# Moving the q and k fetches between the two spreads of the score operands in the sync queue of an attention and MoE kernel

## The chip, the cores and the metric

One core of one Trainium2 chip. The metric is device microseconds of one launch, the median of three runs. Engines are named as the profile names them: PE (TensorE matmuls), PEld (its weight loads), DVE (VectorE), ACT (ScalarE), POOL (GpSimd), SP (SyncE, which here only issues DMAs). "SPq" in a row is SP's queue of DMA issues.

## The reference

```python
scores = (1/sqrt(D)) * q @ k.T                     # batch 4, 8 heads, 576 rows, D = 64, fp32
bias   = -(cum[:, :, :, None] - cum[:, :, None, :])   # cum = cumsum(max(s, 0))
scores = where(causal, -1e9, scores + minimum(bias, 0))
attn   = softmax(scores)                           # sum + 1e-9
x      = (attn @ v) as 2304 tokens x 512
e      = argmax(x @ w_gate)                        # one of 8 experts per token
y      = gate * sigmoid(x @ w_output_gate) * (relu(x @ w1[e]) @ w2[e])
out    = relu(y @ w_in)**2 @ w_out                 # 512 -> 2048 -> 512
```

## The kernel before

The launch has two parts. The first (up to about 250 us) is attention with the routing; the second is the experts and the last two layers, in which PE is busy almost without a gap. The change is in the first.

Attention works on 16 pairs of heads, pair `pp` = 0 to 15. For every pair the scores need two operand tiles of 128 partitions, one per head: `sta` (three buffers, `st_a`, L312) and `stb` (two buffers, `st_b`, L313). PE transposes q and k (L404, L408), ACT and DVE write high and low parts into `sta` (L434, L438), and then DMAs within the on-chip memory bring the halves to the partitions where the score matmuls (L490) want them:

- **spread b** (`spread_b`, three moves at L441, 576 + 144 + 144 KB) fills `stb` from `sta`;
- **spread a** (`spread_a`, two moves at L441, 144 KB each) copies within `sta`. It writes rows that spread b reads, so its issue waits until spread b has landed;
- `load_aug` (L393, L394) brings four rows of the cumulated bias for each head, ahead of spread b for `stb`, behind spread a for `sta`.

The first score matmul of a pair, `s<-sta` with 68 partitions and 192 columns, needs the last of these, `sta<-aug_d`. In front of it stand only the older instructions of PE.

`load_qk` (L353, L356) fetches raw q and k of a pair from HBM, four DMAs: q and k of 256 KB, and the tails of q and k of 32 KB. They have two buffers each, so the fetch for pair pp waits until POOL has reordered (L373) those of pair pp-2. `load_v` (L380, L383) fetches v in three DMAs, and `store_x` (L726, L730) writes attention's output of an older pair in two. From pair 8 on the first expert's weights come in between, 256 KB a time (`part_load`, `stg`, L253), and ACT rounds them (L257).

All these DMAs are issued by SP, one after another. The order is fixed by numbers: `at(key, function, ...)` collects every step with a key in units (seven units are the seven score blocks of a pair), and each engine gets its instructions in the order of the keys. With `t0 = 7 * pp - 7`, `early` = 7 from pair 5 on, and the table `K_`:

```python
at(max(t0 + K_["ldqk"] - early(pp), t0 - 2 * NU + K_["scq"] - early(pp - 2) + 0.2), load_qk, pp)
tb = t0 + max(K_["dup"], K_["qk"][2] + K_["qkl"] - early(pp) + 0.4)   # t0 - 2.9 from pair 3 on
at(tb - 0.05, load_aug, pp, 1)
at(tb, spread_b, pp)
at(tb - K_["dup"] + K_["dupa"], spread_a, pp)                         # t0 + 0.6 from pair 3 on
at(tb - K_["dup"] + K_["dupa"], load_aug, pp, 0)
```

Of the kernel before, what the change touches and what calls it, by code (L numbers as in the profile page):

```python
# [48 lines left out]
    LE=1.22,  # L49
    LV=0.63,  # L50
    vact=[[0], [1], [1], [1], [0], [1], [1, 1]],
    ldqk=-13.2,
    ldv=-3.41,
    scq=-4.19,
    sck=-5.35,
# [1551 lines left out]
```

## Time and profile before

| | |
|---|---|
| median of 3 runs | 932.81 us (929.98 to 934.12) |
| the profiled execution | 931.6 us, its span 929.7 us |
| PE busy in the span | 867.6 us (93%), 5397 matmuls |
| DVE, ACT, POOL busy | 528.6, 446.3, 283.8 us |
| granted clock of PE, mean | 0.975 |
| DMA, mean | 133 GB/s, 123.87 MB |

All times below are in microseconds from the start of the span of this one execution. A row of a timeline gives the start, the duration, the engine, the line and what was done (x2: two instructions merged in one row), and in brackets the idle time just before it with what ended that. SP's own durations are the time an issue took, not the transfer.

### The profile page before, as it was taken

Reading aid. Unit: us, or ns where it says so; the run is one execution under the profiler, and the core shown is the slowest. Engines: PE = TensorE matmul, PEld = TensorE weight load, DVE = VectorE, ACT = ScalarE, POOL = GpSimd, SP = SyncE. Lnnn points to the kernel's source line nnn. Section 1 sums busy time; section 2 is a strip of 40 time slices with the busy share of each in tenths; the row PEclk is TensorE's granted clock in tenths of the full one; section 3 lists DMA queues with packets and bytes.
Section 4 is the critical chain, followed back from the end, with each engine's and each line's share of the span. In section 5 each row is a group of like instructions: output and inputs, shape, how many; then the busy total and the mean of one; then the engine's idle time right before and its main releaser. Section 6 shows DMA issues by size and latency. Waiting matters only on the chain.

```text
span 929.7 us, 15091 instructions
## 1 busy us (share of the span) xinstructions
PE 867.6 (93%) x5397; PEld 761.8 (82%) x5397; DVE 528.6 (57%) x1166; ACT 446.3 (48%) x985; POOL 283.8 (31%) x311
## 2 busy tenths in 40 slices
PE   7999998889989999998987899999999999999992
PEld 5777766667589989998987798999999999989991
DVE  8777666667758787887695666332323322322220
ACT  6677677778436556555654444232322323222220
POOL 5333143532236577767540244011001001001001
PEclk9999899999999999999998999999999999999996
DMA  5667677777158888888966642220000100000001
GB/s 151 160 155 177 164 172 193 188 191 187 37 181 277 253 251 282 279 232 271 305 221 195 199 151 71 68 68 15 25 29 35 35 1 35 1 1 35 1 1 37
DMA packets 87572, 123.87 MB, mean 133 GB/s; under 512 B 33601, under 2 KB 58177, under 8 KB 86594
## 3 DMA queue, kind: packets, MB, share of 16 engines
q1 hardware_dynamic: 80978, 103.77, 40.4%
q0 software_dynamic: 6224, 18.01, 5.4%
q10 hardware_dynamic: 288, 1.05, 0.4%
q8 instruction: 45, 0.74, 0.3%
q14 instruction: 37, 0.30, 0.1%
HBM read 83.12 MB, written 23.17 MB: 114 GB/s over the span
## 4 chain that ended last, share of the span: by engine, by line
PE 32%; issue 30%; DMA 16%; ACT 6%; DVE 5%; POOL 4%; SPq 3%; POOLq 0%; DVEq 0%; ACTq 0%
PE z L1196 10%; PE z L1241 6%; DMA stb<-sta 4%; PE z L1234 3%; PE s L490 3%; DMA cv<-in_moe_w_in_dram 3%; PE t L588 3%; PE t L550 2%; DVE w L238 2%; ACT p L534 2%; POOL out_dram L1273 2%; DMA sta<-aug_d 1%; DMA cv<-in_moe_w_out_dram 1%; DMA stg<-in_moe_w_dram 1%; SPq L441 1%
## 5 line engine op out<-in xcount | busy, mean ns | idle before, releaser
L1196 PE MATMUL z<-xt,w 128*128 128x384 f32 (+6 forms) x1920 | 338.5, 325 | 6.3 <-DVE r L1214 3.0
L1196 PEld LDWEIGHTS z<-xt,w 128*128 128x128 f32 x1920 | 316.0, 190 | 16.3 <-DVE h L1208 3.4
L1241 PE MATMUL z<-w,h 128*128 128x512 f32 x864 | 214.9, 393 | 0.0
L1241 PEld LDWEIGHTS z<-w,h 128*128 128x128 f32 x864 | 160.7, 188 | 29.3
L1214 DVE SCALAR_TENSOR_TENSOR r<-z,r 128x384 f32<-128x384 f32 x96 | 53.3, 555 | 168.2 <-ACT r L1213 168.2
L1213 ACT ACTIVATE r<-z 128x384 f32<-128x384 f32 x96 | 47.0, 490 | 168.2 <-PE z L1196 166.4
L1234 PE MATMUL z<-h,w 128*128 128x304 f32 (+5 forms) x768 | 117.6, 302 | 8.2 <-ACT h L1207 5.9
L1234 PEld LDWEIGHTS z<-h,w 128*128 128x128 f32 x768 | 109.6, 191 | 9.4 <-ACT h L1207 6.3
L238 DVE TENSOR_TENSOR w<-stg,w 128x1024 fp32r<-128x1024 f32 x72 | 109.8, 1525 | 8.5 <-ACT w L234 8.2
L1273 POOL DMA_INDIRECT out_dram<-ysb,tok_m x18 | 17.4, 964 | 314.7 <-ACT ysb L1260 312.4
L234 ACT CAST w<-stg 128x1024 fp32r<-128x1024 f32 x72 | 75.5, 1049 | 70.5 <-DMA stg<-in_moe_w_dram 50.0
L1217 DVE TENSOR_TENSOR h<-r,h 128x384 fp32r<-128x384 f32 x96 | 56.7, 590 | 55.6 <-ACT h L1216 55.6
L534 ACT ACTIVATE p<-p,nm 128x128 f32<-128x128 f32 (+3 forms) x144 | 84.3, 590 | 4.2 <-DVE nm L517 4.1
L517 DVE CUSTOM_DVE_ANT_0 p<-s,mask 128x128 f32<-128x128 f32 (+3 forms) x128 | 59.8, 486 | 45.9 <-PE s L490 45.0
L1216 ACT CAST h<-r 128x384 fp32r<-128x384 f32 x96 | 49.3, 513 | 73.4 <-DVE r L1214 73.4
L1178 POOL TENSOR_TENSOR cvm<-cvm,cva 128x512 f32<-128x512 f32 x32 | 44.1, 1377 | 100.3 <-DVE cva L1177 59.1
L550 PE MATMUL t<-ident,p 128*128 128x128 f32 x400 | 69.5, 289 | 2.1 <-ACT pt L569 0.7
L490 PE MATMUL s<-sta 68*128 68x192 f32 (+7 forms) x204 | 51.7, 350 | 14.9 <-DMA sta<-aug_d 13.2
L550 PEld LDWEIGHTS t<-ident,p 128*128 128x128 f32 x400 | 47.1, 145 | 15.3 <-ACT p L534 7.2
L1179 POOL TENSOR_TENSOR cvm<-cvs,cvm 128x512 f32<-128x512 f32 x32 | 58.9, 1841 | 2.5
L588 PE MATMUL t<-pt,v 128*64 128x320 f32 (+4 forms) x448 | 53.1, 368 | 0.0
L569 ACT COPY pt<-t 128x512 f32<-128x512 f32 (+1 forms) x94 | 46.8, 514 | 12.2 <-PE t L550 7.1
(218 smaller groups left out, 957.3 us busy)
## 6 DMA issues: line engine op xcount, KB each, us to landing
stg<-in_moe_w_dram SPq DMA_DIRECT2D x56, 512.0 KB
cv<-in_moe_w_out_dram SPq DMA_DIRECT2D x16, 512.0 KB
stb<-sta SPq DMA_DIRECT2D x14, 576.0 KB
cv<-in_moe_w_in_dram SPq DMA_DIRECT2D x14, 512.0 KB
xr<-yT_d SPq DMA_DIRECT2D x6, 768.0 KB
q<-in_q_dram SPq DMA_DIRECT2D x16, 256.0 KB
k<-in_k_dram SPq DMA_DIRECT2D x16, 256.0 KB
v<-in_v_dram SPq DMA_DIRECT2D x32, 128.0 KB
```

The lines of the kernel that those rows point to most:

```text
L234: nc.scalar.copy(out=w_parts(job)[0], in_=raw[job])
L238: nc.vector.tensor_tensor(out=lo, in0=raw.pop(job), in1=hi.bitcast(F32), op=ALU.subtract)
L490: nc.tensor.matmul(ps[0:mw, d0:d0 + nn], lhsT=ql[r, m0:m0 + mw], rhs=kl[r, c0:c0 + nn], start=(i == 0 and (tail or n == 0)), stop=(done an ...
L517: nc.vector.tensor_tensor_reduce(out=dst, in0=src, in1=msk, scale=-1.0, scalar=3.0e38, op0=ALU.add, op1=ALU.min, accum_out=nm[:, c:c + 1])
L534: nc.scalar.activation(out=pt[:, cs], in_=pt[:, cs], func=AF.Exp, scale=-1.0, bias=nm[:, c:c + 1], accum_out=rs[:, r:r + 1])
L550: nc.tensor.transpose(tp[:, i * P:(i + 1) * P], pt[:, j0:j0 + P], ident)
L588: nc.tensor.matmul(o[64 * hd:64 * hd + 64, c0:n], lhsT=vt[r0:P, jb, hd, :], rhs=pt[r0:P, hd, jb, c0:n], start=(jb == 0), stop=(jb == last))
L1179: nc.gpsimd.tensor_tensor(out=m, in0=sq, in1=m, op=ALU.add)
L1196: nc.tensor.matmul(ps[:, 0:n], lhsT=wa[:, zw, kk, fl * P:(fl + 1) * P], rhs=xt[:, zx, kk, 0:n], start=(i == 0), stop=(i == 3 * KD - 1))
L1217: nc.vector.tensor_tensor(out=ht[:, 1, 0:n], in0=gg, in1=ht[:, 0, 0:n].bitcast(F32), op=ALU.subtract)
L1234: nc.tensor.matmul(y_acc[g][d][:, 0:n], lhsT=wb[:, zw, fl, d * P:(d + 1) * P], rhs=ht[:, zh, 0:n], start=(f == 0 and i == 0), stop=(f == n ...
L1241: nc.tensor.matmul(acc, lhsT=ht[:, zh, c * P:(c + 1) * P], rhs=wb[:, zw, fl, :], start=(f == 0 and i == 0), stop=(f == nf - 1 and i == 2))
```

## The change

One number of the table: the key of the q and k fetch.

```diff
-    ldqk=-13.2,
+    ldqk=-16.83,
```

From pair 5 on the key of the fetch for pair pp goes from t0 - 20.2 towards t0 - 23.83. Counted from the pair three earlier, whose t0 is 21 units less, that is from t0 + 0.8 (behind its spread a at t0 + 0.6) to t0 - 2.83 (behind its spread b at t0 - 2.9). The instructions of PE, DVE, ACT and POOL keep their order; on SP the fetches of pairs 6 to 15, 40 DMAs, change place, ten times the same way. The fetches of the pairs before stay where they are.

SP at pair 6, with the fetch for pair 9 (`stb_136`, `sta_133` are the buffers of pair 6):

```order
 L441 DMA stb_136<-sta_133 64x576 x2
+L353 DMA q<-in_q_dram 128x2x256
+L356 DMA q<-in_q_dram 64x2x64
+L353 DMA k<-in_k_dram 128x2x256
+L356 DMA k<-in_k_dram 64x2x64
 L441 DMA sta_133<-sta_133 64x576 x2
 L393 DMA sta_133<-aug_d 4x576
 L394 DMA sta_133<-aug_d 4x576
-L353 DMA q<-in_q_dram 128x2x256
-L356 DMA q<-in_q_dram 64x2x64
-L353 DMA k<-in_k_dram 128x2x256
-L356 DMA k<-in_k_dram 64x2x64
```

The four fetches went from behind the bias rows of `sta` to the place between the last move of spread b and the first of spread a.

SP at pair 9, where weights (`stg`) are fetched too, behind the last move of spread b:

```order
+L353 DMA q<-in_q_dram 128x2x256
+L356 DMA q<-in_q_dram 64x2x64
+L353 DMA k<-in_k_dram 128x2x256
+L356 DMA k<-in_k_dram 64x2x64
 L253 DMA stg<-in_moe_w_dram 128x512
 L441 DMA sta_133<-sta_133 64x576 x2
 L393 DMA sta_133<-aug_d 4x576
 L394 DMA sta_133<-aug_d 4x576
-L353 DMA q<-in_q_dram 128x2x256
-L356 DMA q<-in_q_dram 64x2x64
-L353 DMA k<-in_k_dram 128x2x256
-L356 DMA k<-in_k_dram 64x2x64
```

Here a weight fetch stood between the spreads already; the fetches of q and k now stand ahead of it too.

SP at pair 2 of the kernel before, which has this order of the fetches already, and keeps it:

```order
L441 DMA stb_136<-sta_135 64x576 x2
L353 DMA q<-in_q_dram 128x2x256
L356 DMA q<-in_q_dram 64x2x64
L353 DMA k<-in_k_dram 128x2x256
L356 DMA k<-in_k_dram 64x2x64
L441 DMA sta_135<-sta_135 64x576 x2
L393 DMA sta_135<-aug_d 4x576
L394 DMA sta_135<-aug_d 4x576
L380 DMA v<-in_v_dram 128x4x64 x2
```

Nothing moved here: it is the one place of the kernel before where q and k are fetched between the spreads.

## Rows read from the trace of the kernel before

**Rows 1.** Waits of PE, 30 to 245 us: total, times, longest.

```profile
PE s L490 <- DMA sta<-aug_d: 13.2, 7, 2.8
```

**Rows 2.** Waits of SP's queue, whole span: total, times, longest.

```profile
SPq L441 <- DMA stb<-sta: 20.9, 14, 2.6
...
SPq L353 <- POOL qr L373: 4.6, 1, 4.6
...
SPq L393 <- PE s L490: 2.5, 7, 0.5
```

**Rows 3.** Timeline of SP, one cycle: the DMAs around pair 6.

```profile
86.70 0.43 SPq L393 DMA_DIRECT2D stb<-aug_d  x1
...
87.58 3.60 SPq L441 DMA_DIRECT2D stb<-sta  x3
93.19 1.10 SPq L441 DMA_DIRECT2D sta<-sta  x2
...
94.92 0.25 SPq L394 DMA_DIRECT2D sta<-aug_d  x1
95.26 0.39 SPq L353 DMA_DIRECT2D q<-in_q_dram  x1
...
97.79 1.09 SPq L380 DMA_DIRECT2D v<-in_v_dram  x2
...
99.63 0.54 SPq L726 DMA_DIRECT2D x_d<-xs  x1
...
100.83 0.43 SPq L393 DMA_DIRECT2D stb<-aug_d  x1
```

**Rows 4.** Timeline of PE: the first score matmul of pairs 3, 6, 8, 11, 12, 13.

```profile
54.95 0.45 PE L490 MATMUL s<-sta 68*128 68x192 f32 x2
...
96.89 0.45 PE L490 MATMUL s<-sta 68*128 68x192 f32 x2 [1.68 <-DMA sta<-aug_d]
...
126.38 0.45 PE L490 MATMUL s<-sta 68*128 68x192 f32 x2 [1.58 <-DMA sta<-aug_d]
...
172.85 0.46 PE L490 MATMUL s<-sta 68*128 68x192 f32 x2 [2.69 <-DMA sta<-aug_d]
...
189.19 0.45 PE L490 MATMUL s<-sta 68*128 68x192 f32 x2 [2.42 <-DMA sta<-aug_d]
...
204.68 0.45 PE L490 MATMUL s<-sta 68*128 68x192 f32 x2
```

**Rows 5.** Stretches: length, busy us (instructions) of PE, PEld, DVE, ACT, POOL; clock, DMA share, GB/s.

```profile
86.70:100.83 14.13, 12.39 (x87) 9.24 (x86) 8.96 (x33) 9.21 (x27) 2.83 (x4) 0.91 0.73 170
...
206.00:217.81 11.81, 11.76 (x91) 8.78 (x89) 8.99 (x37) 10.35 (x31) 2.55 (x2) 1.00 0.84 200
...
98.00:105.20 7.20, 7.20 (x35) 5.54 (x33) 5.07 (x22) 5.12 (x17) 3.85 (x5) 0.53 0.83 198
```

**Rows 6.** Timeline of SP around pair 2, whose fetch stands between the spreads already.

```profile
28.92 0.44 SPq L393 DMA_DIRECT2D stb<-aug_d  x1
...
29.80 3.71 SPq L441 DMA_DIRECT2D stb<-sta  x3
33.60 0.72 SPq L353 DMA_DIRECT2D q<-in_q_dram  x1
...
36.55 1.18 SPq L441 DMA_DIRECT2D sta<-sta  x2
...
38.76 2.17 SPq L380 DMA_DIRECT2D v<-in_v_dram  x2
...
42.94 0.41 SPq L393 DMA_DIRECT2D stb<-aug_d  x1
```

**Rows 7.** Timeline of SP, pair 9: weights between the spreads.

```profile
136.37 0.83 SPq L253 DMA_DIRECT2D stg<-in_moe_w_dram  x1
138.35 1.10 SPq L441 DMA_DIRECT2D sta<-sta  x2
```

**Rows 8.** Timeline of ACT: a rounding of weights that waited for their fetch.

```profile
155.72 0.62 ACT L257 CAST w<-stg 128x512 fp32r<-128x512 f32 x1 [1.49 <-DMA stg<-in_moe_w_dram]
```

## The prediction

> **What bounds the kernel now.** I read the waits of PE first, since PE is busy 93% of the span and what it waits for is what can be won. In the attention part one wait stands out: the first score matmul of a pair waits for `sta<-aug_d`, 13.2 us in 7 times [rows 1]. The timeline of PE shows where: at pair 6 it sat 1.68 us, at pair 8 1.58, at pair 11 2.69, at pair 12 2.42, and from pair 13 on it does not wait [rows 4]. So up to pair 12 PE runs at the pace at which the operand `sta` arrives.
>
> Then the timeline of SP, which issues that DMA. One cycle of it, from one `stb<-aug_d` to the next, is 100.83 - 86.70 = 14.13 us, and in this time SP is idle once: spread b is issued from 87.58 to 91.18, and spread a starts only at 93.19, 2.0 us later [rows 3]. The waits of SP say the same for all pairs: 20.9 us for `stb<-sta` in 14 times, and next to nothing for PE, which must free `stb` (2.5 us in 7 times, never over 0.5) [rows 2]. SP does not wait for the compute engines, they wait for SP: **its queue is the bound of pairs 3 to 12.** Where the table has no q and k to fetch, the cycle falls to 217.81 - 206.00 = 11.81 us and PE is busy 11.76 of it [rows 5].
>
> Of the 16 DMA engines the same rows show a mean share of 0.73 in the 14.13 us cycle and of 0.84 in the 11.81 us one [rows 5]. So the transfers have room: 0.73 x 14.13 = 10.3 us of full work per cycle would fit a 12.3 us cycle at the share of 0.84.
>
> The Trainium skill speaks against this reading: "DMA: Bandwidth & Descriptors", section "Issuing engines are not separate DMA queues", says that the time a sequencer takes to initiate a DMA is usually small relative to the DMA itself. By that rule the order of issues could change nothing, since the bytes are the same. This trace does not agree: 14.13 - 2.0 = 12.1 us of a cycle are issues.
>
> **The change, step by step.** It adds and removes nothing; 40 issues (ten fetches of four) go from behind spread a to the place between the spreads. Each engine but SP keeps its order.
>
> *Removed: the idle time in front of spread a.* The ten pairs 3 to 12 get a fetch there. The four others of the 14 do not change: pair 2 has it already, and pairs 13 to 15 have the weight fetch alone, whose gap is 138.35 - (136.37 + 0.83) = 1.15 us [rows 7]. That leaves 20.9 - 3 x 1.15 = 17.5 us in ten waits, 1.75 us each.
>
> *Cost of the fetch at the new place.* Behind spread a its four issues took 97.79 - 95.26 = 2.53 us [rows 3]; at pair 2, between the spreads, 36.55 - 33.60 = 2.95 us, and spread a followed with no wait [rows 6]. So it covers the mean wait of 1.75 whole, and costs 0.42 us more. In a cycle SP saves 1.75 - 0.42 = 1.33 us, and spread a itself, counted from spread b, is issued 2.95 - 1.75 = 1.2 us later (at pair 12, whose wait I take as the longest, 2.6 of rows 2, only 0.35).
>
> *Cost in the DMA engines.* Spread a now stands behind 576 KB of q and k. No row prices that at its new place. Least: nothing, since the engines are idle after spread b lands and the fetch is partly through before spread a is issued. Most: the whole time of the fetch, 2.5 us. I take 0.3 us, near the low end: pair 2 in this order has its operand in time [rows 6], and the weight fetch of 256 KB between the spreads costs SP no more than 0.83 us at its place [rows 7].
>
> *Cost behind it.* The next issue is v. In the one place with this order its two large DMAs took 2.17 us instead of 1.09 [rows 3, 6]. If that came with the order, 1.1 us of the saving would go each time. I take it as a chance event, since the issue of v at pair 6 was at full speed with the same fetch just ahead of it, and count it in a rival. The weight fetch slips behind q and k by 2.95 us; ACT waits for it already, 1.49 us once [rows 8], while PE is waiting too. Since SP runs earlier by more than this after two or three cycles, I count nothing; without that cover ACT would hold PE for up to 3 us per pair in pairs 9 to 12.
>
> *The other queues.* The fetch waits for POOL to free the buffer. The only such wait of the whole span is one of 4.6 us [rows 2], and it comes before pair 2. So SP should not be held there.
>
> *Sum.* Every pair from 8 to 12 finds PE waiting, so the time of pair 12 is set by SP. Nine cycles lie before its spread a: 17.5 - 2.6 = 14.9 us of waits saved, less 9 x 0.42 = 3.8, is 11.1 us; less 0.35 for its own later issue and 0.3 in the engines is 10.5 us. Is PE able to follow? From pair 3 to pair 12 it took 189.19 - 54.95 = 134.2 us [rows 4], of it 13.2 waiting: 121.0 us of work. 134.2 - 10.5 = 123.7 us is more than that, so 2.7 us of waits stay, and the gain is whole. Behind pair 12 PE does not wait, so what is won there stays won to the end.
>
> One more part is PE's clock. After the wait of 1.68 us at pair 6 the granted clock went to half: from 98.0 to 105.2 us the mean is 0.53, that is 1.2 GHz for nearly all of it, at full busy [rows 5]. Up to 3.6 us of work are lost in such a stretch. SP sets the pace, so I count it as slack for PE and not in the sum; it is in the lower end of the range.
>
> The profiled execution took 931.6 us; 931.6 - 10.5 = 921.1. It lies 1.2 us under the median of the three runs, 932.8, against which the same gain gives 922.3. I predict **922 us**.
>
> **Rivals.**
>
> *1. SP's saving is eaten (no change).* For it: the cycle at pair 2, in the new order, is 42.94 - 28.92 = 14.02 us, hardly less than 14.13 [rows 3, 6], since the issue of v took 1.1 us more. Against it: that is one cycle, in the first pairs, with all else faster. If it comes each time: 14.9 - 9 x (0.42 + 1.08) = 1.4, less 0.65, is a gain of 1 us: 932. The skill's rule above, the transfers as the bound, would give 932 too. Together 0.23.
>
> *2. The fetch holds up spread b, and v stalls (slower).* The engines work on q and k while spread b is still moving. If its landing slips by the whole 2.5 us of the fetch, spread a is issued at 95.7 instead of 93.19, and what follows starts where it did before: the cycle stays at 14.13, and PE gets each operand 2.5 us later. With the stall of v on top every cycle is 1.1 us longer: 2.5 + 10 x 1.1 = 13.5 us, 946. The point that decides is whether fetch and v together cost SP more than the 1.75 us wait that they replace. Against it: spread a followed the fetch at once at pair 2, 6.75 us after spread b began, where 5.6 is usual [rows 3, 6]. 0.16.
>
> *3. PE comes free altogether (faster still).* If the landing is not held at all and the slow clock goes, all 13.2 us of waits and some 3.6 of the clock come back: 932.8 - 16.8 = 916. Against it: SP's cycle in the stretch with weights stays long. 0.11.
>
> *4. The fetch is held by POOL, so the change does not do what it says.* SP would then stand in front of spread a. For it only the 4.6 us of rows 2, at one time. It is within rival 2.
>
> **How the numbers follow.** The forecast, gains of 5 to 14 us, has 0.50. With rival 3 faster is 0.61, no change 0.23, slower 0.16; about 0.5%, 4.7 us, is what a measurement of this kernel can tell from no change. The range reaches from 913 us, a little under rival 3, to 936 us, 3 us over the median, which takes in rival 1 and the one-time part of rival 2 (2.5 us). What is left out is mainly the rest of rival 2. The forecast's own range is 918 to 928.
>
> **What would show it.** Right: in SP's timeline the gap behind spread b is gone, spread a follows the k fetch within about 0.1 us, the cycle of pairs 4 to 7 is near 12.8 us, the wait for `stb<-sta` falls from 20.9 to about 4 us, and PE's wait for `sta<-aug_d` from 13.2 to about 3. Wrong: the wait for `stb<-sta` is still there behind the fetch (rival 2), v's two DMAs take 2 us in most cycles (rival 1), the idle time of PE moves to ACT's rounding of weights, or SP waits at L353 for POOL.

## The result and the profile after

Beside four runs of the kernel before on the same chip (median 933.46 us, 929.98 to 934.75), the changed kernel took **921.62 us** in the median of four runs (918.72 to 923.04): a ratio of 0.9878, with a 95% interval of 0.9843 to 0.9914. That is 11.8 us faster. The profiled execution took 923.04 us, its span is 921.2 us.

SP's waits after the change, whole span (total, times, longest):

```profile
SPq L353 <- POOL qr L373: 5.5, 3, 4.6
...
SPq L441 <- DMA stb<-sta: 3.6, 3, 1.4
...
SPq L441 <- ACT sta L434: 1.6, 4, 0.7
...
SPq L393 <- PE s L490: 1.5, 4, 0.4
```

Set beside [rows 2], the wait for `stb<-sta` went from 20.9 us in 14 times to 3.6 in 3. The wait for POOL at L353 still has its one long case of 4.6 us, and in total it grew by only 0.9. SP does not start to wait for PE's score matmuls either: 1.5 us, from 2.5. The largest new wait is one for ACT, which writes `sta`: 1.6 us in 4 times. So the removed wait has no successor of its size on SP.

SP's timeline at pair 6 after the change (start, duration, line, DMA):

```profile
81.16 0.43 SPq L393 DMA_DIRECT2D stb<-aug_d  x1
...
82.04 3.54 SPq L441 DMA_DIRECT2D stb<-sta  x3
85.68 0.79 SPq L353 DMA_DIRECT2D q<-in_q_dram  x1
...
88.74 2.26 SPq L441 DMA_DIRECT2D sta<-sta  x2
...
91.57 0.29 SPq L394 DMA_DIRECT2D sta<-aug_d  x1
91.96 0.94 SPq L380 DMA_DIRECT2D v<-in_v_dram  x2
...
94.89 0.44 SPq L393 DMA_DIRECT2D stb<-aug_d  x1
```

Against [rows 3]: the q fetch starts 0.10 us behind the end of spread b, where 2.0 us stood empty, and spread a follows the fetch. The cycle is 94.89 - 81.16 = 13.73 us, from 14.13. It is the longest of pairs 3 to 8, because the two moves of spread a took 2.26 us to issue here, against 1.10 in [rows 3]. The v DMAs took 0.94 us.

What PE waits for in the attention part, 30 to 245 us (total, times, longest), the longest two rows:

```profile
PE s L490 <- DMA sta<-aug_d: 7.0, 6, 1.7
PE s L490 <- DVE pt L571: 1.6, 1, 1.6
```

The wait of [rows 1] fell from 13.2 us to 7.0, in 6 times. The second row is new, one wait for the DVE at pair 15. The first score matmuls show where the 7.0 us are; these are the ones of pairs 3, 6, 9, 12 and 13 (in brackets the idle time before it and what ended it):

```profile
54.77 0.45 PE L490 MATMUL s<-sta 68*128 68x192 f32 x2
...
93.57 0.45 PE L490 MATMUL s<-sta 68*128 68x192 f32 x2
...
135.82 0.45 PE L490 MATMUL s<-sta 68*128 68x192 f32 x2 [1.34 <-DMA sta<-aug_d]
...
177.58 0.45 PE L490 MATMUL s<-sta 68*128 68x192 f32 x2 [1.50 <-DMA sta<-aug_d]
...
191.88 0.45 PE L490 MATMUL s<-sta 68*128 68x192 f32 x2
```

Beside [rows 4]: pair 6 does not wait any more, pair 12 starts 189.19 - 177.58 = 11.6 us earlier, pair 13 12.8 us earlier. Of the 7.0 us, 5.5 are the waits of pairs 9 to 12 (1.34, 0.96, 1.69, 1.50), where weights are fetched too. The rest are pairs 7 and 8 (1.02, 0.51).

Busy time by engine, granted clock, DMA share and GB/s in two stretches: 35 to 205 us, most of the attention part, and the stretch in which routing goes over into the experts. First the kernel before, then the changed one:

```profile
35.00:205.00 170.00, 155.38 (x1184) 116.74 (x1179) 114.78 (x395) 122.27 (x351) 62.45 (x73) 0.96 0.74 176
```

```profile
35.00:205.00 170.00, 161.56 (x1279) 121.19 (x1276) 125.42 (x432) 132.65 (x383) 65.60 (x75) 1.00 0.81 192
243.90:254.00 10.10, 8.30 (x30) 6.29 (x31) 5.86 (x28) 2.00 (x5) 1.17 (x3) 0.50 0.17 46
```

In the same 170 us the profile has 1279 matmuls of PE instead of 1184. The clock is full (1.00, 2.4 GHz) where it was 0.96, and the DMA engines are busy 0.81 of the time instead of 0.74. Later, from 243.9 to 254.0 us, the clock was at half (0.50, 1.2 GHz) in this execution. That stretch matters below.

### The profile page after: what moved, and what is told of

It reads as the page before. It is cut to its first block, busy times and chain, and to the rows that moved or that the text cites. A ratio compares the mean times of both kernels' runs of the same rounds, so it can differ in the third digit from the quotient of the medians.

```text
span 921.2 us, 15063 instructions
## 1 busy us (share of the span) xinstructions
PE 865.7 (94%) x5397; PEld 761.8 (83%) x5397; DVE 532.7 (58%) x1166; ACT 445.5 (48%) x985; POOL 283.7 (31%) x311
## 4 chain that ended last, share of the span: by engine, by line
PE 37%; issue 31%; DMA 9%; DVE 6%; POOL 5%; ACT 5%; SPq 3%; POOLq 0%; DVEq 0%; ACTq 0%
PE z L1196 13%; PE z L1241 6%; PE z L1234 5%; PE t L588 3%; PE s L490 3%; PE t L550 2%; DVE w L238 2%; DMA w_out_d<-cvm 2%; POOL out_dram L1273 2%; ACT p L534 2%; DMA cv<-in_moe_w_in_dram 1%; DMA xr<-x_d,tbl_p 1%; SPq L441 1%; DMA sta<-aug_d 1%; PE t L404 1%
## 5 line engine op out<-in xcount | busy, mean ns | idle before, releaser
L1196 PE MATMUL z<-xt,w 128*128 128x384 f32 (+6 forms) x1920 | 340.9, 327 | 6.4 <-DVE h L1208 4.2
L1196 PEld LDWEIGHTS z<-xt,w 128*128 128x128 f32 x1920 | 318.2, 192 | 16.2 <-DVE h L1208 4.5
L238 DVE TENSOR_TENSOR w<-stg,w 128x1024 fp32r<-128x1024 f32 x72 | 112.4, 1561 | 10.0 <-ACT w L234 9.7
L550 PE MATMUL t<-ident,p 128*128 128x128 f32 x400 | 67.1, 280 | 1.6 <-ACT pt L569 0.7
L550 PEld LDWEIGHTS t<-ident,p 128*128 128x128 f32 x400 | 45.2, 141 | 14.6 <-ACT p L534 6.8
```

The costliest lines, as they stand in the source:

```text
L238: nc.vector.tensor_tensor(out=lo, in0=raw.pop(job), in1=hi.bitcast(F32), op=ALU.subtract)
L550: nc.tensor.transpose(tp[:, i * P:(i + 1) * P], pt[:, j0:j0 + P], ident)
L1196: nc.tensor.matmul(ps[:, 0:n], lhsT=wa[:, zw, kk, fl * P:(fl + 1) * P], rhs=xt[:, zx, kk, 0:n], start=(i == 0), stop=(i == 3 * KD - 1))
```

## The experiments

The theory, and what stood against it. The expectations name some of them by letter:

- **Q**, the theory: SP's queue is the bound, and the gain is the empty time behind spread b, filled with issues that have to be made anyway.
- **E**: the gain comes from q and k arriving earlier.
- **T** (the transfers): what counts is how the DMA engines are loaded, which the order in SP's queue only shifts. Two of the expectations call it C.
- **K**: the gain is the clock, which no longer falls in the attention part.
- **A**: what remains is a wait of ACT for the weights.

**The fetch still earlier, but with the gap left empty.** The whole fetch goes ahead of spread b:

```diff
-    ldqk=-16.83,
+    ldqk=-16.98,
```

> The fetch of q and k one step earlier still (-16.98): ahead of the bias rows and of spread b, so it does not fill the gap between the spreads. Theory Q (SP's queue is the bound, and the gain is the idle gap that is filled): the gap is back, the wait for stb<-sta near the 20.9 us of before; one fetch more stands ahead of each operand, 2.5 us once; time 932 to 936 us. Rival E (the gain comes from q and k being there earlier): the fetch is earlier than in the changed kernel by another 4 us, so 922 us or less.

Measured: 933.72 us (10 runs) beside 933.83 (23 runs), a ratio of 1.0009 [0.9984, 1.0034]. SP's wait and its timeline at pair 6 of this kernel:

```profile
SPq L441 <- DMA stb<-sta: 21.6, 15, 3.0
```

```profile
89.50 0.44 SPq L393 DMA_DIRECT2D stb<-aug_d  x1
...
90.38 3.80 SPq L441 DMA_DIRECT2D stb<-sta  x3
96.87 1.10 SPq L441 DMA_DIRECT2D sta<-sta  x2
```

The gap is back: spread b's issue ends at 94.18 and spread a starts at 96.87, and the sum of waits is 21.6 us, that of the kernel before. The fetch comes even earlier than in the changed kernel, and the whole gain is gone. That rules out E as the cause, and it is the clearest run of the study, since between this kernel and the changed one only the place of the fetch differs: ahead of spread b and its bias rows, or behind them. It does not rule out T by itself, because the transfers of q and k change their place among the others too; at pair 6 the gap is 2.7 us here, from 2.0.

**Another issue in the gap, with q and k at their old place.** The kernel before, with the two stores of `x_d` moved between the spreads:

```diff
-    sx=2.42,
+    sx=2.55,
```

> The kernel before with its fetch where it was, and the store of attention's output (two issues, 1.2 us) moved from ahead of spread b into the gap. Theory Q: SP saves about 1.15 us in each of ten cycles whatever fills the gap, and spread b starts 1.2 us earlier besides: gain some 11 us, 920 to 925 us; the wait for stb<-sta falls from 20.9 to 5 to 10 us. Rival E (early fetch): nothing changes, 932 us. Rival C (the transfers are the bound, and the gain came from the fetch standing elsewhere among them): within 3 us of 932.

Measured: 927.19 us (8 runs), ratio 0.9924 [0.9901, 0.9947], 6.6 us faster. That is a little over half of the change's gain, and less than the 920 to 925 us expected. SP's wait, PE's wait, and SP's timeline at pair 7:

```profile
SPq L441 <- DMA stb<-sta: 0.4, 2, 0.2
```

```profile
PE s L490 <- DMA sta<-aug_d: 6.5, 4, 2.3
```

```profile
95.65 3.61 SPq L441 DMA_DIRECT2D stb<-sta  x3
99.36 0.74 SPq L726 DMA_DIRECT2D x_d<-xs  x1
100.14 0.81 SPq L730 DMA_DIRECT2D x_d<-xs  x1
101.19 1.21 SPq L441 DMA_DIRECT2D sta<-sta  x2
```

So a filler that has nothing to do with q and k empties the wait as well (20.9 to 0.4 us) and halves that of PE. That is what Q says, and 6.6 us are more than the 3 that rival C allowed. The size I had wrong. In pairs 9 to 13, where SP does not wait behind them, the stores cost 1.67 to 1.81 us in the gap, some 0.5 us more than the 1.2 at their old place, so less of each gap is won. PE's waits have a second cause here: at pairs 9 and 11 the operand came 4.5 and 4.1 us behind the issue of its last row, from 2.1 in the kernel before. How the shortfall divides between the two was not tried. With the wait of pairs 3 to 12 gone here too, the gain is little over half, so the emptied wait alone does not give its size.

**Both in the gap.** The changed kernel with the same edit of `sx`:

> The changed kernel with the store moved into the gap as well. Theory Q: the gap is filled by the fetch alone already, so nothing is left to save: within 2 us of the changed kernel, 920 to 924 us. Were there idle time left (the gap not yet filled) the store would win another 5 us or more, 917; were the transfers ahead of spread a what holds it, its landing would slip by another 1 us each and the time would be 925 or more.

Measured: 925.87 us (10 runs), ratio 0.9926 [0.9897, 0.9954]. In the medians that is about 4 us slower than the changed kernel, and more than the 920 to 924 us expected by Q; the intervals of the two ratios overlap, so the loss is likely and not shown. PE's wait, and the first and the last row of the filled gap:

```profile
PE s L490 <- DMA sta<-aug_d: 7.3, 6, 3.3
```

```profile
96.45 3.65 SPq L441 DMA_DIRECT2D stb<-sta  x3
...
104.65 1.24 SPq L441 DMA_DIRECT2D sta<-sta  x2
```

The six issues hold SP from 100.10 to 104.65, 4.55 us, where about 2 us were empty. Spread a, for which PE waits, is issued that much later, and PE's longest wait is 3.3 us instead of 1.7. What fills more than the gap delays the next operand, and the change had filled it already. Whether that accounts for all of the 4 us I did not settle; the expectation had put 925 us or more down to the transfers ahead of spread a, and this run does not tell the two apart.

**Only q in the gap.** The changed kernel with the k fetch left at the old -13.2, so that only q moves:

```diff
-            def load_qk(pp, engs=(nc.sync, nc.sync)):
+            def load_qk(pp, nms="qk", engs=(nc.sync, nc.sync)):
...
+                    if nm not in nms:
+                        continue
...
-                    at(max(t0 + K_["ldqk"] - early(pp), t0 - 2 * NU + K_["scq"] - early(pp - 2) + 0.2), load_qk, pp)
+                    for nm, ld in (("q", K_["ldqk"]), ("k", -13.2)):
+                        at(max(t0 + ld - early(pp), t0 - 2 * NU + K_["scq"] - early(pp - 2) + 0.2), load_qk, pp, nm)
```

> The changed kernel with only the two DMAs of q in the gap, those of k behind spread a as before. Theory Q (SP's queue is the bound, the filled gap is the gain): q's issues take 1.5 us there and leave 0.3 to 0.5 us of the wait in pairs without weights, but spread a is issued 1.3 us sooner after spread b: the two nearly cancel, 920 to 924 us. Rival T (what stands among the transfers ahead of spread a is a large cost): half of it gone, 917 to 919 us. Rival E (early fetch): k comes as late as before, POOL needs k first, so most of the gain is lost, 928 us or more.

Measured: 923.0 us (10 runs) beside 932.13 (20 runs), ratio 0.9909 [0.9876, 0.9942]. SP's wait (L443 is L441 of the others) and PE's:

```profile
SPq L443 <- DMA stb<-sta: 6.8, 11, 1.1
```

```profile
PE s L492 <- DMA sta<-aug_d: 4.6, 5, 1.5
```

Half of the fetch brings most of the gain, 9.1 us. Two issues fill two thirds of the empty time (20.9 to 6.8 us), and the longest that is left is 1.1. A pair needs q and k both, so with k as late as before E gives no gain here. The run speaks for Q again.

**The weights off SP's queue.** In the changed kernel, the fetches of `part_load` are issued by POOL:

```diff
-        nc.sync.dma_start(out=t, in_=src[:, h * 512:(h + 1) * 512] if key[1] == "a" else src[:, h, :])
+        nc.gpsimd.dma_start(out=t, in_=src[:, h * 512:(h + 1) * 512] if key[1] == "a" else src[:, h, :])
```

> The changed kernel with the 16 weight fetches of the attention part issued by POOL's queue instead of SP's: the same bytes at about the same places, two issues (1.2 us) less for SP in each cycle from pair 8 on. Theory Q: SP's cycle there falls from about 14.4 to about 13.1 us, PE's waits for sta<-aug_d from 7.0 to 1 to 3 us, gain 3 to 5 us: 917 to 919 us. Rival C (transfers): the bytes ahead of spread a are the same, so within 1.5 us of 921.6.

Measured: 921.77 us (4 runs, 915.8 to 925.8), ratio 0.9858 [0.9801, 0.9915]. A second set of runs of the same kernel, whose label promises more than it holds (only the weights go by POOL in it):

> The variant with the weights issued by POOL once more, beside it: it takes 1.2 us of issues from each of SP's cycles from pair 8 on, and PE hardly waits for the operand there either. If SP is no longer the bound once the wait of PE is gone, it can bring no more than the other: 918 to 921 us, the two within 2 us. If SP's issues were still the bound, 2 us or more faster than the other.

Measured: 922.8 us (6 runs), ratio 0.9894 [0.9863, 0.9924]. Waits of PE in the first and in the second:

```profile
PE s L490 <- DMA sta<-aug_d: 2.9, 2, 2.4
```

```profile
PE s L490 <- DMA sta<-aug_d: 4.6, 5, 1.4
```

I expected 917 to 919 us from it, and missed; the time is the one that rival C forecast. PE waits 2 to 4 us less than in the changed kernel, and the time does not fall. The profiles show more than the time. The first expert matmuls (L1196: count, shortest, median and longest in ns, then the first and the last start) of the changed kernel, of the first and of the second set:

```profile
L1196 PE MATMUL z<-xt,w x96: 320/323/854, 251.0 to 279.7; 128*128 128x352 f32 x96
```

```profile
L1196 PE MATMUL z<-xt,w x106: 308/323/512, 248.1 to 279.9; 128*128 128x352 f32 x96, 128*128 128x320 f32 x10
```

```profile
L1196 PE MATMUL z<-xt,w x96: 320/323/509, 247.9 to 278.1; 128*128 128x352 f32 x96
```

The experts start 3 us earlier, and the rest of the span takes 921.4 - 248.1 = 673.3 us and 923.0 - 247.9 = 675.1 instead of 921.2 - 251.0 = 670.2 (667.8 in the second profile of the changed kernel). So taking the weights off SP's queue does shorten the attention part, and in these executions the part behind it gives that back. Why, stays open, and the run does not show that SP's queue has stopped being the bound of attention.

**The weights behind spread a.** In the changed kernel every second weight fetch goes from between the spreads to behind spread a:

```diff
-                at(tw - 5.0, part_load, *job)
+                at(tw - 5.0 + (1.7 if i % 2 else 0.0), part_load, *job)
```

> The changed kernel with the weight fetch that stands between the spreads (pairs 9 on) moved behind spread a and its bias rows. In the changed kernel's trace the operand lands 3.4 to 3.8 us after the last issue in pairs 9 to 11, where it was 2.1 before. If that is the weights and q and k standing ahead in the rings, it falls to 2.0 to 2.6 us, PE's waits for sta<-aug_d fall from 7.0 to 2 to 4 us, and the time is 918 to 921 us. Rival A: the roundings on ACT, which wait for these weights, wait longer and hold PE instead: 922 us or more.

Measured: 919.85 us (5 runs), ratio 0.9859 [0.9815, 0.9902]; the same kernel in a later set of runs:

> The variant with the weights behind spread a once more, with more rounds: its PE waits for sta<-aug_d fell to 0.9 us, 6 us less than in the changed kernel, but the time by only 1 to 2 us, inside the interval. If the operand's wait is now off PE's path and PE's own work is the bound, 918 to 920.5 us. If the first result was chance, 921 to 922.5.

Measured: 920.11 us (6 runs) beside 931.59 (10), ratio 0.9873 [0.9841, 0.9905]. First SP at pair 9 of the changed kernel, then the same place in this one with PE's score matmul of the pair, and PE's wait:

```profile
129.63 0.59 SPq L253 DMA_DIRECT2D stg<-in_moe_w_dram  x1
...
132.03 0.34 SPq L394 DMA_DIRECT2D sta<-aug_d  x1
```

```profile
131.92 0.33 SPq L394 DMA_DIRECT2D sta<-aug_d  x1
```

```profile
133.95 0.47 PE L490 MATMUL s<-sta 68*128 68x192 f32 x2
```

```profile
PE s L490 <- DMA sta<-aug_d: 0.9, 2, 0.5
```

In the changed kernel PE starts pair 9 at 135.82, 3.79 us behind the issue of the last operand row. Here it starts 133.95 - 131.92 = 2.03 us behind it, and without waiting. Over the attention part PE's wait for `sta<-aug_d` goes from 7.0 us to 0.9, and to none in the second run (1.4 us for the moves of spread a, `sta<-sta`, came there instead). The transfers of q, k and weights that stand ahead of the operand together hold it up by up to 1.8 us: there T is right, for the pairs with weights. Either of the two alone does not: with q and k ahead it is 2.03 us here, with weights ahead 2.07 to 2.16 in the kernel before. The time is not shown to be better than that of the changed kernel, since the intervals overlap; the experts start at 250.7 us in the first run and at 247.7 in the second, from 251.0. New waits of PE for ACT take part of it (1.8 us at L626 in the first of the two), and ACT's own wait for weights grows from 3.7 us to 5.9 and 5.5 in the two, as A has it, though only here.

**The clock kept full in the kernel before.** Two to six matmuls without use are put ahead of the first score matmul of seven pairs, so that PE does not idle there. The score matmul overwrites what they leave:

```diff
+                if u == 0:
+                    for _ in range({4: 2, 6: 4, 8: 4, 9: 2, 10: 6, 11: 6, 12: 6}.get(pp, 0)):
+                        nc.tensor.matmul(
+                            ps, lhsT=onesb, rhs=onesb.unsqueeze(1).to_broadcast([P, 512 // P, P]), start=True, stop=True)
```

> The kernel before with idle matmuls (two to six of 0.38 us, their result overwritten) just ahead of the first score matmul of the seven pairs in which PE waits, so that PE is busy for most of each wait; nothing else is changed. If SP sets the pace up to pair 12 and the slow clock of PE (6.8 us of work lost in the attention part of the kernel before) is slack, as the prediction has it: 930 to 934 us. Rival K (the clock is a main part of the gain): 5 us or more faster, 928 us or less.

Measured: 929.1 us (11 runs), ratio 0.9979 [0.9955, 1.0002], 3 us faster in the median, which falls between the two theories. SP's wait, and the stretch from 35 to 205 us in its windows:

```profile
SPq L441 <- DMA stb<-sta: 18.9, 14, 2.1
```

```profile
35.00:205.00 170.00, 161.68 (x1249) 118.66 (x1247) 122.57 (x415) 126.86 (x369) 63.73 (x74) 1.00 0.76 182
```

The clock is full there, as in the changed kernel, and 3 of the 11.8 us come with it, 4.2 by the end of the interval. SP's wait stays. So K is not the whole gain, though it may be a part of it; the interval still holds no change, and the profiled execution, the fastest of the eleven, differs from the one before in more than the clock (its v DMAs had no slow issue).

**The changed kernel again,** on the same chip as the runs with q alone, with the weights behind spread a and with the full clock:

> The changed kernel itself, so that the other variants of the call have it beside them on the same chip: 919 to 924 us, by every theory.

Measured: 920.67 us (5 runs) beside 932.13 (20), ratio 0.9893 [0.9848, 0.9938]. Its row for the start of the experts, and PE's first score matmul of pair 12:

```profile
243.00:254.00 11.00, 8.89 (x45) 6.56 (x46) 5.95 (x28) 2.00 (x5) 2.35 (x4) 0.84 0.22 66
```

```profile
180.30 0.45 PE L490 MATMUL s<-sta 68*128 68x192 f32 x2
```

The same code keeps the clock at 0.84 there, where the first profile had 0.50, and its span is 918.7 us instead of 921.2. Pair 12 starts 2.7 us later than in the first profile, without a wait.

## Why the prediction was right, and which terms were off

The median is 921.62 us for 922 predicted, and the gain of 11.8 us stands beside a sum of 10.5. The mechanism was right; that the numbers lie so close is in part luck, as the steps show:

- **SP's queue is the bound of pairs 3 to 12: right.** With the gap filled by q and k, by q alone or by stores, the kernel is faster by 11.8, 9.1 and 6.6 us; with the fetch still earlier and the gap empty it is as slow as before. It no longer holds to the end of that stretch once the gap is filled: in the second profile of the changed kernel PE starts pair 12 without a wait, 4.9 us behind the issue of the last operand row.
- **17.5 us of waits removed: right.** 20.9 - 3.6 = 17.3 us; forecast were about 4 us left. One row was misread: the longest wait of [rows 2], 2.6 us, is that of pair 3 (spread b's issue ends at 47.38, spread a starts at 50.04); pair 12's was 2.4. In the sum the two places where it is used cancel.
- **The fetch costs 2.95 us at the new place: nearly right.** At pair 6 it is 88.74 - 85.68 = 3.06 us, over the ten pairs 2.66 to 3.35, against 2.53 behind spread a.
- **A cycle near 12.8 us in pairs 4 to 7: a little off.** They took 12.99, 13.20, 13.73 and 13.36 us. The forecast subtracted the mean saving from pair 6, which has one of the shortest cycles of the kernel before (14.1 to 15.0 in these pairs). The saving itself was right: the nine cycles of pairs 3 to 11 took 164.47 - 42.02 = 122.45 us instead of 177.25 - 42.94 = 134.31, which is 1.32 each, 1.33 forecast.
- **0.3 us in the DMA engines: nearly right at pair 12, where the sum counts it, and mis-sized at pairs 9 to 11.** Without weights the operand comes as fast as before: pair 8 starts 2.06 us behind the issue of its last row, pair 6 of the kernel before 96.89 - 94.92 = 1.97. With them it takes 3.79 us at pair 9, and 3.4 and 3.46 at the two pairs behind it, against 2.07 to 2.16 in the kernel before: 1.2 to 1.7 us. At pair 12 it is 177.58 - 175.14 = 2.44 us against 1.99, 0.45 more. The Trainium skill says in "DMA: Bandwidth & Descriptors", section "Queues, rings and completion order", that each DMA engine takes descriptors in the order of its ring. By that rule the operand has to stand behind q, k and the weights, and the trace agrees: taking one weight fetch out of its way brings 3.79 back to 2.03 us.
- **The sum at pair 12: right, with luck.** In the two profiles PE starts pair 12 by 11.6 us and 8.9 us earlier than before, 10.5 forecast. Of the 11.6, 0.9 was there before pair 3 (42.02 for 42.94), most of it at v of pair 2, whose order did not change: its issues took 2.24 us and not 2.96. In the second profile SP is as early (its last row at 175.36, from 187.20), and PE's own work sets the start.
- **2.7 us of PE's waits stay: wrong, 7.0 stayed.** The step that failed is "121.0 us of work". Those microseconds held work at half clock, as at 98 to 105 us [rows 5]. With the gaps gone the clock did not fall between 35 and 205 us in this execution (in the second profile of the same code it was 0.98), so the same work took 177.58 - 54.77 - 7.0 = 115.8 us. PE became faster by 5.2 us, and waits for the operand with it. In the second profile the same work took 180.30 - 55.00 - 6.6 = 118.7 us, faster by 2.3. In the first profile SP and the landing set the pace up to pair 12, so this slack hardly moves the time, and the forecast held.
- **v's issue stays at full speed: right.** It is 0.94 to 0.99 us from pair 3 on, so the 2.17 us at pair 2 [rows 6] came with something else; the kernel before has the like in its old order, 2.02 us at pair 8 and 1.75 at pair 9. Rival 1 has nothing left.
- **ACT is not held by later weights: right.** Its roundings wait 3.7 us for the stage buffer in 4 times, 4.7 in 5 before.
- **What is won stays won: right for attention, loose behind it.** Pair 15 starts 11.9 us earlier, the first expert matmul (L1196) 261.64 - 251.00 = 10.6, and the span ends 929.7 - 921.2 = 8.5 earlier in the two profiled executions. The stretch at half clock at 244 us is a part of that: the first 36 expert matmuls took 7.50 us in it, and 6.15 in the second profile. The second profile of the same code ends 11.0 us earlier than before, and its clock is higher there. That the clock makes the whole difference was not tried. The two sets with the weights issued by POOL lose more behind attention: the experts start 3 us earlier, and the span does not end earlier.

The rule of the Trainium skill that I set against the reading ("DMA: Bandwidth & Descriptors", section "Issuing engines are not separate DMA queues": issue time is usually small beside the DMA itself) would, as I worked it out, have given no change. This case's runs disagree with that working: the same bytes in another order of issue took 11.8 us less, and the order with the gap left empty gave it all back.

Of the rivals, the landing of spread b did not slip (rival 2): spread a follows the fetch at once, and the cycles of pairs 3 to 7 (12.95 to 13.73 us) are each shorter than those they replace (14.09 to 15.20). PE did not come free either (rival 3): in the two sets of runs where its wait all but vanished, the time fell to 919.85 and 920.11 us, not to 916. What bounds the changed kernel beyond that was not settled. POOL did not hold the fetch.

No version tried is shown to be faster than the changed kernel.

## What to carry to other kernels

In a queue that issues in order, a wait for an earlier DMA of the same queue to land is time in which other issues cost little (here the four of a fetch took about 0.5 us more than elsewhere). Look for it by the releaser of the queue's waits, and put there independent issues that take as long as the wait; a longer filling delays the issue of what stands behind it. Then look at the time from the last issue of an operand to its consumer: what was put ahead of it in the queue can hold it up in the DMA engines too, as q and k together with weights did here. And when PE's work between two points is taken from a trace with waits, take out the stretches at low clock first, since they may go with the waits. At the end look at where the part that was changed now ends, and not at the time alone: with the weights issued by POOL attention ended 3 us earlier, and the time did not fall.

## What the runs showed of the hardware

- Issues right behind the large spread b are slower than the same issues elsewhere: the four of q and k 2.66 to 3.35 us in the ten pairs of the changed kernel against 2.53, the two stores 1.67 to 1.81 against about 1.2. I had taken the single case of pair 2, 2.95 us, for this price, and nine of the ten pairs lie at it or above.
- Now and then an issue takes about 1 us longer, in different places: v at pairs 2, 8 and 9 of the kernel before, 2.17, 2.02 and 1.75 us for 1.09; spread a at pair 6 of the changed one, 2.26 for 1.10. No run ties it to an order of the queue.
- The same code has its stretches of half clock in different places in two executions: at 243.9 to 254.0 us throughout in one, for a part of it (0.84 in the mean) in the other, and the spans differ by 2.5 us.
